# w1's last 64 rows on 16 partitions, by one transfer with an outermost dimension of 4

## The chip, the cores and the metric

The kernel runs on one core of one Trainium2 chip. The metric is the device time of one execution in microseconds (us); lower is better.

## The reference, cut to what matters

The result is `x + A(xn) + B(xn)`. A is a decode attention over a window of 2048 keys and values (16 K and 16 V transfers of 2 MB each in the kernel; they are most of the 88.5 MB read). B is a small MLP, and the change is in its first matrix, w1:

```python
h = _gelu(_layernorm(x, axis=-1) @ w1)          # x: 4 x 1 x 576, w1: 576 x 576
c = D // 4
g0 = jnp.pad(h[:, :, 0*c:1*c], ((0, 0), (1, 0), (0, 0)))[:, :S, :]
...                                             # g1, g2, g3 likewise: shifts along S by 1 and 2
hs = jnp.concatenate([g0, g1, g2, g3], axis=-1) @ w2
x1 = x + hs
h2 = _gelu(_layernorm(x1, axis=-1) @ w3) @ w4
```

S is 1 here. A shift by one or two positions leaves padding alone, so `hs` is zero whatever h is. The kernel nevertheless loads w1 and w2 and computes h and hs. Two things follow. The output can't tell whether h is right, so the correctness test says nothing of the new layout of w1. And in an experiment h may be wrong while the output stays right.

## The kernel before: the parts that matter

All large transfers are issued by SP on one queue, in the order of the `key` at the end of each line; in the trace each large one has 16 landings, one for each of the core's 16 DMA engines, and each engine works through its own share of the queue without a gap (its next packet starts 3 to 4 ns before the last one ends). Of each 576-row matrix, 512 rows fill 128 partitions with four rows each; the last 64 rows ("rag") are interleaved on the even and the odd partitions of a shared tile.

```python
def rag_pair(tile, even, odd):
    return [(tile[p:128:2, 0:w.shape[1]], w[512:576, :]) for p, w in enumerate((even, odd))]
...
ev_wq = [add_dma([(kt_t[:], A_wq[0:512, :].rearrange("(p r) n -> p (r n)", r=4))], "wq", (), -60),
         add_dma(rag_pair(ragq3, B_w3, A_wq), "wqr", ["ragq3_zero"], -59)]
ev_r12 = add_dma(rag_pair(rag12, B_w1, B_w2), "r12", (), -58.5)
ev_w2 = add_dma([(w2main, B_w2[0:512, :].rearrange("(p r) n -> p r n", r=4))], "w2", (), -58)
ev_w3 = add_dma([(w3_t[:], B_w3[0:512, :].rearrange("(p r) n -> p (r n)", r=4))], "w3", (), -57)
ev_w1 = add_dma([(w1main, B_w1[0:512, :].rearrange("(p r) n -> p r n", r=4))], "w1", (), -56)
...                                 # then K0 to K15, V0 to V15, wo, and w4 in five pieces
def pe_h(h):                        # x @ w1, for one half of the columns
    def f(e):
        for r in range(4):
            e.matmul(HTps[h], lhsT=xn2T[:, r, :], rhs=w1main[:, r, HALF * h:HALF * (h + 1)], start=(r == 0), stop=False)
        return e.matmul(HTps[h], lhsT=xn2T[:, 4, :], rhs=rag12[:, HALF * h:HALF * (h + 1)], start=False, stop=True)
    return f
```

Of the kernel before, what the change touches and what calls it, by code (L numbers as in the profile page):

```python
# [7 lines left out]
BF16 = mybir.dt.bfloat16  # L8
# [27 lines left out]
def bass_parallel_sum__sliding_block_cached__mixer_s_mlp__decode_kernel(  # L36
    nc, A_x, A_k_cache, A_v_cache, A_wq, A_wo, B_x, B_w1, B_w2, B_w3, B_w4, out
):
    B, Sq, D = A_x.shape
# [14 lines left out]
    HALF = D // 2  # L54
# [5 lines left out]
    with ExitStack() as ctx:  # L60
        def sb(name, shape, dt):
            return ctx.enter_context(nc.sbuf_tensor(name, shape, dt))
# [7 lines left out]
        w4_t = sb("w4", [128, 36 * D], BF16)  # L70
# [15 lines left out]
        w2main = w4_t[:, 4 * D:8 * D].rearrange("p (r n) -> p r n", r=4)  # L86
        rag12 = w4_t[:, 8 * D:9 * D]
        ragq3 = w4_t[:, 9 * D:9 * D + F]

        x_sb = sb("x_sb", [B, D], BF16)  # L90
        stats = sb("stats", [B, 3, 2, 6], FP32)
# [6 lines left out]
        x1n_bf = sb("x1n_bf", [B, D], BF16)  # L98
        ragsrc = sb("ragsrc", [B, 3, 128], BF16)
        xnT = sb("xnT", [128, 5, 32], BF16)  # L100
        xn2T = sb("xn2T", [128, 5, B], BF16)
        x1nT = sb("x1nT", [128, 5, 32], BF16)
        hs_inT = sb("hs_inT", [128, 5, B], BF16)
        h_sb = sb("h_sb", [B, D], BF16)
# [6 lines left out]
        ident_bf = sb("ident_bf", [128, 128], BF16)  # L111
# [20 lines left out]
        ps = ctx.enter_context(nc.psum_tensor("ps", [128, 8, 512], FP32))[:]  # L132
# [11 lines left out]
        H2Tb = ps[:, 6, :].bitcast(BF16)[:, 0:128]  # L144
        HSps = [ps[0:B, k, 0:HALF] for k in range(2)]
        HTps = [ps[0:B, 2 + k, 0:HALF] for k in range(2)]
        XTps = [ps[:, k, a:a + 10].bitcast(BF16).rearrange("p (c b) -> p c b", b=B) for k, a in ((3, 300), (7, 0), (7, 12))]

        S = {}
        for nm in ("pe", "dve", "act", "pool"):  # L150
# [5 lines left out]
        def add(engine, emit, waits=(), sig=None, key=0.0, inc=(), loop=None, cond=None):  # L156
            seqc[0] += 1
            prog[engine].append(Op(emit, waits, sig, key, seqc[0], inc, loop, cond))

        def tok(nm):  # L160
            if nm not in S:
                S[nm] = sem("t_" + "_".join(str(k) for k in (nm if isinstance(nm, tuple) else (nm,))))
            return nm
# [6 lines left out]
        def add_dma(pairs, skey, waits=(), key=0.0, engine="sp"):  # L170
            tok(skey)
            dma_count[skey] = dma_count.get(skey, 0) + 16 * len(pairs)

            def emit(e):
                for o_, i_ in pairs:
                    e.dma_start(o_, i_).then_inc(S[skey], 16)  # L176
            add(engine, emit, waits, None, key)
            return ("dma", skey, dma_count[skey])

        def rag_pair(tile, even, odd):  # L180
            return [(tile[p:128:2, 0:w.shape[1]], w[512:576, :]) for p, w in enumerate((even, odd))]
# [6 lines left out]
        P = lambda *a, **k: add("pool", *a, **k)  # L188

        def pool_ident(t, tag, pattern, view, key):  # L190
            P(lambda e: e.memset(t[:], 1.0), sig=tag + "1", key=key)
            P(lambda e: e.affine_select(out=view, in_=view, compare_op=ALU.is_equal, fill=0.0, base=0,
                                        pattern=pattern, channel_multiplier=1), waits=[tag + "1"], sig=tag, key=key + 0.5)
        P(lambda e: e.memset(ragq3[:, Hq * Dh:F], 0.0), sig="ragq3_zero", key=-101)
        P(lambda e: e.memset(zeros_bf[:], 0.0), sig="zeros_bf", key=-100)
        pool_ident(ident_bf, "ident_bf", [[-1, 128]], ident_bf[:], -99)
        P(lambda e: e.memset(ragsrc[:], 0.0), sig="rag_zero", key=-97)
        P(lambda e: e.memset(Qpad_t[:], 0.0), sig="qpad_zero", key=-96)
# [12 lines left out]
            waits=["ident_f"], sig="mU", key=-8)  # L211
        for x in range(2):
# [3 lines left out]
        ev_x = add_dma([(x_sb[:], x2)], "x", ["sqrt_table"], -100, engine="act")  # L216
        ev_wq = [add_dma([(kt_t[:], A_wq[0:512, :].rearrange("(p r) n -> p (r n)", r=4))], "wq", (), -60),
                 add_dma(rag_pair(ragq3, B_w3, A_wq), "wqr", ["ragq3_zero"], -59)]
        ev_r12 = add_dma(rag_pair(rag12, B_w1, B_w2), "r12", (), -58.5)
        ev_w2 = add_dma([(w2main, B_w2[0:512, :].rearrange("(p r) n -> p r n", r=4))], "w2", (), -58)  # L220
        ev_w3 = add_dma([(w3_t[:], B_w3[0:512, :].rearrange("(p r) n -> p (r n)", r=4))], "w3", (), -57)
        ev_w1 = add_dma([(w1main, B_w1[0:512, :].rearrange("(p r) n -> p r n", r=4))], "w1", (), -56)
# [32 lines left out]
        def ln_ops(idx, src, dst, first_waits, tag, k0):  # L255
            add("dve", lambda e: (e.bn_stats(out=stats[:, idx, 0, :], in_=src[:, 0:HALF]),
                                  e.bn_stats(out=stats[:, idx, 1, :], in_=src[:, HALF:D]))[1],
                waits=first_waits, sig=f"{tag}_st", key=k0)
            add("dve", lambda e: e.bn_aggr(out=mv[:, idx, :], in_=stats[:, idx].rearrange("p a s -> p (a s)")),  # L259
                waits=[f"{tag}_st"], sig=f"{tag}_mv", key=k0 + 0.01)  # L260
            add("act", lambda e: e.activation(out=sd[:, idx:idx + 1], in_=mv[:, idx, 1:2], func=ACTF.Sqrt, bias=EPS, scale=1.0),  # L261
                waits=[f"{tag}_mv"], sig=f"{tag}_sd", key=k0 + 0.02)
            add("dve", lambda e: e.reciprocal(out=rstd[:, idx:idx + 1], in_=sd[:, idx:idx + 1]),
                waits=[f"{tag}_sd"], sig=f"{tag}_rstd", key=k0 + 0.03)
            add("dve", lambda e: e.tensor_scalar(out=dst[:], in0=src[:], scalar1=mv[:, idx, 0:1], scalar2=rstd[:, idx:idx + 1],
                                                 op0=ALU.subtract, op1=ALU.mult), waits=[f"{tag}_rstd"], sig=f"{tag}_n", key=k0 + 0.04)
            odd = int(idx == 0)
            add("dve", lambda e: e.tensor_copy(out=ragsrc[:, idx, odd:128:2], in_=dst[:, 512:D]), waits=[f"{tag}_n", "rag_zero"], sig=tag, key=k0 + 0.05)  # L268

        def pe_xT(src, idx):  # L270
            def f(e):
                v = src[:, 0:512].rearrange("b (p r) -> b r p", r=4)
                for r in range(4):
                    e.transpose(XTps[idx][:, r, :], v[:, r, :], ident_bf[0:B, 0:B])  # L274
                return e.transpose(XTps[idx][:, 4, :], ragsrc[:, idx, :], ident_bf[0:B, 0:B])
            return f

        ln_ops(0, x_sb, xn_bf, [ev_x], "ln1", -40)
        ln_ops(1, xn_bf, xn2_bf, ["ln1"], "ln2", -30)
        add("pe", pe_xT(xn_bf, 0), waits=["ident_bf", "ln1"], sig="xT", key=-40)  # L280
        add("dve", lambda e: e.tensor_copy(out=xnT[:, :, 0:B], in_=XTps[0]), waits=["xT", "xnT_zero"], sig="xnT", key=-39)

        def pe_q(r):
            def f(e):
# [25 lines left out]
        for b in range(B):  # L310
            add("dve", lambda e, b=b: e.tensor_copy(out=qp_out[:, b], in_=qp_in[:, b]), waits=["qTp", "qpad_zero"],
                sig="qT" if b == B - 1 else None, key=-29.4)
        add("pe", pe_xT(xn2_bf, 1), waits=["ln2", "ident_bf"], sig="x2T", key=-36)
        add("dve", lambda e: e.tensor_copy(out=xn2T[:], in_=XTps[1]), waits=["x2T"], sig="xn2T", key=-25)

        def pe_zero(e):
            ins = None
# [37 lines left out]
        for c in range(NC):  # L355
            lp = ("K", c // NPOS)
            for k in range(NBLK):
# [4 lines left out]
                eng, f = evac(NBLK * c + k)  # L362
                add(eng, f, waits=[f"T{NBLK * c + k}"] + ([f"SC{c - 2}"] if c >= 2 else []), inc=[("evA" if eng == "act" else "evD", 1)],
                    key=NBLK * c + k + 0.2)
            add("pe", pe_SC(c - 1), waits=[take("qs")], sig=f"SC{c - 1}", key=NBLK * c + SC_AFTER + 0.5, loop=lp)
            b, gq = CH[c]
            cc = 4 * b + gq
            P(lambda e, c=c, cc=cc: e.tensor_copy(out=Qs[:, c % NPOS, :], in_=Qpad_t[:, 128 * cc:128 * cc + 128]),  # L368
              waits=["qT", "qs_zero"] + ([f"SC{c - NPOS}"] if c >= NPOS - 1 else []), inc=[("qs", 1)], key=c)
# [6 lines left out]
            waits=["rmax"], sig="negb", key=KS + 0.05)  # L376
        for q in range(4):
            add("act", lambda e, q=q: e.activation(out=P_sb[:, q, :], in_=Sps[:, q, :], func=ACTF.Exp,
                                                   bias=negb[:, 0:1], scale=scale, accum_out=rs4[:, q:q + 1]),
                waits=["negb"], sig=f"exp{q}", key=KS + 0.1 + 0.01 * q)  # L380

        for q in range(4):
            k0 = KS + 0.2 + 0.1 * q
            add("dve", lambda e, q=q: e.transpose(out=PTx[:, q, :], in_=P_sb[:, q, :]), waits=[f"exp{q}"], sig=f"PTx{q}", key=k0)  # L384
            add("pe", lambda e, q=q: e.matmul(ps[:, 4 + q % 3, :], lhsT=permT_bf[:], rhs=PTx[:, q, :], start=True, stop=True),  # L385
                waits=[f"PTx{q}", "permT_bf"] + (["PT0"] if q == 3 else []), sig=f"PTy{q}", key=k0)
            add("act", lambda e, q=q: e.activation(out=PT_t[:, 512 * q:512 * (q + 1)], in_=ps[:, 4 + q % 3, :], func=ACTF.Copy),
                waits=[f"PTy{q}"], sig=f"PT{q}", key=k0 + 0.16)
# [3 lines left out]
            waits=["rinv", "ident_f"], sig="diag", key=KS + 0.82)  # L392
        add("pe", lambda e: e.matmul(rinvps, lhsT=ones_f[:], rhs=diag[:], start=True, stop=True), waits=["diag", "ones_f", "exp3"],
            sig="rinvp", key=KS + 0.9)
        add("dve", lambda e: e.tensor_copy(out=rinvB[:].rearrange("p (c u e) -> p c u e", u=NU, e=2),
                                           in_=rinvps.rearrange("p (u c e) -> p c u e", u=NU, e=2)),
            waits=["rinvp"], sig="rinvB", key=KS + 1.5)
# [20 lines left out]
        for c in range(NC):  # L418
            w = [f"PV{c - 2}"] if c >= 2 else [f"PT{q}" for q in range(4)] + ["mU_bf1"]
            b, gq = CH[c]  # L420
            add("dve", dve_pad(c), waits=w, inc=[(tok("pad"), 1)], key=KV + 2 * max(c - 1, 0) + 0.2)
            add("pe", pe_PV(c), waits=[take("pad"), take(("v", c % NPOS), 16)] + ([take("otn")] if b == 0 else []), sig=f"PV{c}",
                key=KV + 2 * c, loop=("V", gq))
            if b == B - 1:
                hv = lambda t, gq=gq: t[:, 0:128].rearrange("p (b h) -> p b h", b=B)[:, :, 8 * gq:8 * gq + 8]
                add("dve", lambda e, hv=hv: e.tensor_tensor(out=hv(OTn), in0=OTps.rearrange("p (b h) -> p b h", b=B), in1=hv(rinvB), op=ALU.mult),  # L426
                    waits=["rinvB", f"PV{c}"], sig=f"OTn{gq}" if gq == 3 else None, inc=[(tok("otn"), 1)] if gq < 3 else [], key=KV + 2 * c + 0.1)
# [13 lines left out]
        def pe_AO(half):  # L441
# [10 lines left out]
            waits=["OTy"], sig="ORp", key=KT - 2.5)  # L452
# [15 lines left out]
        def pe_h(h):  # L468
            def f(e):
                for r in range(4):  # L470
                    e.matmul(HTps[h], lhsT=xn2T[:, r, :], rhs=w1main[:, r, HALF * h:HALF * (h + 1)], start=(r == 0), stop=False)
                return e.matmul(HTps[h], lhsT=xn2T[:, 4, :], rhs=rag12[:, HALF * h:HALF * (h + 1)], start=False, stop=True)
            return f
        for h in range(2):
            add("pe", pe_h(h), waits=[ev_w1, ev_r12, "xn2T", "xnT"], sig=f"hT{h}", key=-3 + 0.1 * h)
# [7 lines left out]
        for h in range(2):  # L483
# [3 lines left out]
                waits=[f"hs{h}", "ln1"], sig="x1" if h else "x1a", key=-29 + 0.6 * h)  # L487
        ln_ops(2, x1_bf, x1n_bf, ["x1"], "ln3", -24)
        add("dve", lambda e: e.tensor_tensor(out=t1[:], in0=x_sb[:], in1=x1_bf[:], op=ALU.add), waits=["x1"], sig="t1", key=-5)
        add("pe", pe_xT(x1n_bf, 2), waits=["ln3", "xn2T"], sig="x1T", key=-23)  # L490
        add("dve", lambda e: e.tensor_copy(out=x1nT[:, :, 0:B], in_=XTps[2]), waits=["x1T", "x1nT_zero"], sig="x1nT", key=-23)
        for h in range(2):
            add("act", lambda e, h=h: e.activation(out=h_sb[:, HALF * h:HALF * (h + 1)], in_=HTps[h], func=ACTF.Gelu_apprx_tanh),
                waits=[f"hT{h}", "x1nT"], sig="gelu_h" if h else None, key=-0.69 + 0.01 * h)

        segs = []
        for g in range(4):
            t = 9 * g
            while t < 9 * g + 9:
                n = next(m for m, (a, z) in enumerate(W4N) if a <= t < z)  # L500
# [18 lines left out]
        for k in range(3):  # L519
            add("act", lambda e, k=k: e.activation(out=h2g[:, 9 * XS[k]:9 * XS[k + 1]], in_=H2ps[k], func=ACTF.Gelu_apprx_tanh), waits=["h2_3"],  # L520
                sig="gelu2" if k == 2 else None, key=-0.9 + 0.1 * k)

        def pe_h2T(e):
# [7 lines left out]
            waits=["h2T"], inc=[("evA", 1)], key=-0.3)  # L531
        add("dve", lambda e: e.tensor_copy(out=h2o[:, :, 8, :], in_=H2Tb.rearrange("p (g y) -> p g y", g=4)[..., 0:B]),
            waits=["h2T"], inc=[("evD", 1)], key=-0.3)
# [112 lines left out]
```

## Time and profile before

The median was 214.85 us of 3 runs (214.82 to 215.07).

| | before | read from |
|---|---|---|
| span | 213.6 us | page |
| DMA engines, mean rate | 415 GB/s | page, part 2 and the DMA line |
| last step of the chain | 32.2 us of DMA, w4 | chain of waits |
| tensor engine busy | 67% | page, part 1 |
| K transfer, issue to landing | 14.5 us | DMA issues |

The page's rows for the DMA in 40 slices of the span (tenths busy, then GB/s), and its DMA line:

```profile
DMA  7999989999999999999999999999999999999993
GB/s 270 418 380 507 442 359 436 417 428 423 426 430 426 423 430 436 422 430 426 433 426 430 430 422 427 430 420 433 430 423 426 430 433 426 426 429 439 422 406 130
DMA packets 6546, 88.65 MB, mean 415 GB/s; under 512 B 764, under 2 KB 1032, under 8 KB 1544
```

The chain that ended last, in order of time (start in us, length in us, what):

```profile
178.05 0.04 issue
178.09 32.22 DMA w<-in_B_w_dram
210.31 0.04 issue
210.36 1.40 PE ps L431 x18
211.75 0.43 DVE out_sb L548
```

The reader is to see two things. The DMA is busy from the second slice to the last but one. And the end waits for the last piece of w4, issued 32 us earlier, which lay behind everything else on the queue. The kernel is bound by the DMA queue: its packets fill 97.8% of the 16 engines' span.

One level lower, the trace records each DMA packet with start, length and size. A packet of one size nearly always took the same time: 51 ns for 1152 B, 178 ns for 4608 B, 611 ns or a little more for 16384 B; the next packet on its engine started 3 to 4 ns before it ended. So each engine's end is the sum of its packets. The engines don't end together: the 16 landings of each transfer late in the run are spread over 2.0 us. This is the table of landings of two transfers, in ns after the first engine's landing (below I call this an engine's phase), computed from the packet records (K0 is the first K transfer, V15 the last V transfer):

```
before, K0  at  33.82 us: 0 31 66 133 159 162 244 289 308 338 389 449 450 451 492 1711
before, V15 at 191.03 us: 0 5 13 155 245 410 427 898 1440 1525 1628 1664 1691 1895 1964 2020
```

Most of the spread comes from fetches of instructions. Queue 8, of the kind "instruction", moved 8 packets of 16 KB, seven of them before the last pieces of w4; each took 1.02 to 1.10 us on one engine, stretched a packet beside it as well, and set that engine back by 1.5 us against the others (1711 in the first row is one: this engine stood at 172 when wq had landed). So each fetch costs time on the DMA engine that carries it among the data; what it costs the engine whose instructions are fetched I did not measure.

### The profile page before, as it was taken

How to read it: one execution, taken by the hardware profiler on the slowest of the kernel's cores; microseconds unless marked ns; L12 is line 12 of the kernel's file. 1: busy time of each engine (PE TensorE's matmuls, PEld its weight loads, DVE VectorE, ACT ScalarE, POOL GpSimd, SP SyncE). 2: the span in 40 equal slices, each digit the busy share in tenths (PEclk: the TensorE clock that was granted, in tenths of full speed). 3: DMA queues.
4: the chain of work that ended last, by engine and by line, in shares of the span. 5: the costliest groups of instructions: out<-in, count | busy, mean ns of one | idle time of the engine just before them, and what ended most of it. 6: DMA issues, size and time to landing. Idle time of an engine off the chain costs nothing. (4 is left out here: it accounts for less than half of the span.)

```text
span 213.6 us, 5903 instructions
## 1 busy us (share of the span) xinstructions
PE 142.3 (67%) x2664; PEld 110.4 (52%) x2668; DVE 75.2 (35%) x147; ACT 61.8 (29%) x76; POOL 10.9 (5%) x38
## 2 busy tenths in 40 slices
PE   0058469999999999999996178033444433336995
PEld 0023256877778887888874058033434433334542
DVE  0332701666666666666664840100010001001000
ACT  2001204666555665666666530000000000000000
POOL 8301000000000000000000000000000000000000
PEclk9999959999999999999999555555555555555799
DMA  7999989999999999999999999999999999999993
GB/s 270 418 380 507 442 359 436 417 428 423 426 430 426 423 430 436 422 430 426 433 426 430 430 422 427 430 420 433 430 423 426 430 433 426 426 429 439 422 406 130
DMA packets 6546, 88.65 MB, mean 415 GB/s; under 512 B 764, under 2 KB 1032, under 8 KB 1544
## 3 DMA queue, kind: packets, MB, share of 16 engines
q1 hardware_dynamic: 6520, 88.50, 97.8%
q8 instruction: 8, 0.13, 0.2%
q14 instruction: 2, 0.02, 0.0%
q10 hardware_dynamic: 16, 0.01, 0.0%
HBM read 88.49 MB, written 0.00 MB: 414 GB/s over the span
## 5 line engine op out<-in xcount | busy, mean ns | idle before, releaser
L333 PE MATMUL ps<-perm_bf,ring 128*128 128x128 bf16 x1024 | 62.5, 219 | 1.3 <-PEq L572 0.3
L333 PEld LDWEIGHTS ps<-perm_bf,ring 128*128 128x128 bf16 x1024 | 57.5, 98 | 10.7 <-issue 10.7
L340 DVE COPY kt<-ps 128x1024 bf16<-128x1024 bf16 x80 | 52.3, 687 | 27.2 <-PE ps L333 27.2
L339 ACT ACTIVATE kt<-ps 128x1024 bf16<-128x1024 bf16 x48 | 49.2, 1024 | 30.8 <-PE ps L333 29.5
L414 PE MATMUL ps<-PTpad,ring 128*128 128x8 bf16 x1024 | 29.6, 168 | 41.2 <-PEq L572 37.6
L414 PEld LDWEIGHTS ps<-PTpad,ring 128*128 128x128 bf16 x1024 | 28.7, 104 | 42.3 <-issue 42.2
L549 ACT ACTIVATE out_sb<-ps 4x288 bf16<-4x288 f32 x1 | 0.4, 402 | 87.2 <-PE ps L431 87.2
L347 PE MATMUL ps<-kt,Qs 128*32 128x512 bf16 x272 | 17.8, 382 | 1.4 <-PEq L572 1.4
L403 DVE TENSOR_TENSOR PTpad<-PT,mU_bf 128x512 bf16<-128x512 bf16 x16 | 6.4, 421 | 29.4 <-PE ps L414 29.4
L426 DVE TENSOR_TENSOR OTn<-ps,rinvB 128x32 bf16<-128x32 f32 x4 | 0.8, 191 | 34.5 <-PE ps L414 34.5
L347 PEld LDWEIGHTS ps<-kt,Qs 128*32 128x32 bf16 x272 | 5.7, 95 | 6.8 <-issue 1.5
L274 PE MATMUL ps<-ident_bf,xn_bf 4*128 4x4 bf16 x8 | 0.6, 170 | 12.9 <-DVE ragsrc L268 12.9
L368 POOL COPY Qs<-Qpad 128x128 bf16<-128x128 bf16 x16 | 4.6, 296 | 86.9 <-PE ps L347 73.6
L511 PE MATMUL ps<-w,x1nT 128*32 128x387 bf16 (+7 forms) x90 | 5.9, 404 | 2.3 <-DMA w<-in_B_w_dram 2.0
L274 PEld LDWEIGHTS ps<-ident_bf,xn_bf 4*128 4x128 bf16 x8 | 0.4, 112 | 12.9 <-issue 10.5
L511 PEld LDWEIGHTS ps<-w,x1nT 128*32 128x32 bf16 x90 | 4.5, 124 | 3.6 <-DMA w<-in_B_w_dram 2.3
L431 PE MATMUL ps<-w,ORT 128*4 128x288 bf16 x64 | 5.5, 345 | 0.4 <-DVE ORT L453 0.4
L548 DVE CAST out_sb<-ps 4x288 bf16<-4x288 f32 x1 | 0.4, 446 | 14.5 <-PE ps L431 14.5
L431 PE MATMUL ps<-w,h2T_sb 128*4 128x288 bf16 x72 | 5.0, 286 | 0.7 <-DMA w<-in_B_w_dram 0.7
L385 PE MATMUL ps<-kt,permT_bf 128*128 128x512 bf16 x3 | 1.8, 607 | 4.9 <-DVE kt L384 4.8
L261 ACT ACTIVATE sd<-mv 4x1 f32<-4x1 f32 x3 | 0.6, 202 | 14.8 <-DVE mv L259 14.8
L431 PEld LDWEIGHTS ps<-w,ORT 128*4 128x4 bf16 x64 | 3.3, 102 | 2.9 <-DVE ORT L453 1.0
(99 smaller groups left out, 65.8 us busy)
## 6 DMA issues: line engine op xcount, KB each, us to landing
ring<-in_A_k_cache_dram SPq DMA_DIRECT2D x16, 2048.0 KB, 14.5
ring<-in_A_v_cache_dram SPq DMA_DIRECT2D x16, 2048.0 KB, 17.4
w<-in_B_w_dram SPq DMA_DIRECT2D x1, 4608.0 KB, 24.0
w<-in_A_wo_dram SPq DMA_DIRECT2D x2, 2304.0 KB, 20.9
kt<-in_A_wq_dram SPq DMA_DIRECT2D x1, 4096.0 KB, 12.3
w<-in_B_w_dram SPq DMA_DIRECT2D x1, 2592.0 KB, 28.0
w<-in_B_w_dram SPq DMA_DIRECT2D x3, 576.0 KB, 13.7
w<-in_B_w_dram SPq DMA_DIRECT2D x1, 1296.0 KB, 30.6
```

The lines of the kernel that those rows point to most:

```text
L274: e.transpose(XTps[idx][:, r, :], v[:, r, :], ident_bf[0:B, 0:B])
L333: ins = e.transpose(tb[n % 4][:, t, :], slot_t(c)[:, 8 * k + t, :], perm_bf[:])
L339: return "act", lambda e: e.activation(out=ktbuf[:, n % 16], in_=tb[n % 4], func=ACTF.Copy)
L340: return "dve", lambda e: e.tensor_copy(out=ktbuf[:, n % 16], in_=tb[n % 4])
L347: ins = e.matmul(Sps[32 * u:32 * u + 32, q, :].rearrange("p (t i) -> p t i", t=16), lhsT=Qs[:, c % NPOS, 32 * u:32 * u + 32], rhs=ktgrp[:, ...
L368: P(lambda e, c=c, cc=cc: e.tensor_copy(out=Qs[:, c % NPOS, :], in_=Qpad_t[:, 128 * cc:128 * cc + 128]), waits=["qT", "qs_zero"] + ([f"SC{ ...
L385: add("pe", lambda e, q=q: e.matmul(ps[:, 4 + q % 3, :], lhsT=permT_bf[:], rhs=PTx[:, q, :], start=True, stop=True), waits=[f"PTx{q}", "pe ...
L403: return lambda e: e.tensor_tensor(out=PTpad[:, c % 2], in0=PTv[:, :, cc, :].unsqueeze(2).to_broadcast([128, NT, NU, 2]), in1=mU_bf[:].uns ...
L414: ins = e.matmul(o_, lhsT=slot_t(c)[:, t, :], rhs=PTpad[:, c % 2, t].rearrange("p u e -> p (u e)"), start=(t == 0), stop=(t == NT - 1))
L426: add("dve", lambda e, hv=hv: e.tensor_tensor(out=hv(OTn), in0=OTps.rearrange("p (b h) -> p b h", b=B), in1=hv(rinvB), op=ALU.mult), waits ...
L431: return e.matmul(ACC[h], lhsT=lhsT, rhs=rhs, start=start, stop=stop, tile_position=(0, 32 * h), skip_group_check=True)
L511: ins = e.matmul(H2ps[k][32 * g:32 * g + 32, :].rearrange("p (x c) -> p x c", c=9)[:, :, off:off + cnt], lhsT=x_, rhs=w[:, base_:base_ + 1 ...
```

## The change

Its intent: replace 64 small packets by 16 large ones that occupy four engines only. Rows are chosen so that partition 4a+b gets the four neighbouring rows 16b+4a to 16b+4a+3, that is 4608 contiguous bytes; the source's outermost dimension is 4. The matmul that consumed 64 (of 128) partitions becomes four matmuls on 16 partitions, and x is transposed to fit. "w3 whole ahead of w1" holds in both kernels: those lines are not touched. The diff, cut to its core:

```diff
+        w1rag = w4_t[0:16, 18 * D:22 * D]
...
-        xn2T = sb("xn2T", [128, 5, B], BF16)
+        xn2T = sb("xn2T", [128, 8, B], BF16)
...
+        P(lambda e: e.memset(rag12[:], 0.0), sig="rag12_zero", key=-98)
...
-        ev_r12 = add_dma(rag_pair(rag12, B_w1, B_w2), "r12", (), -58.5)
+        ev_r12 = add_dma([(w1rag, B_w1[512:576, :].rearrange("(b a c) n -> a b (c n)", b=4, a=4)),
+                          (rag12[1:128:2, :], B_w2[512:576, :])], "r12", ["rag12_zero"], -58.5)
...
+            if idx == 1:
+                r_out = ragsrc[:, idx, 0:64].rearrange("q (c a b) -> q c a b", c=4, a=4)
+                r_in = r_in.rearrange("q (b a c) -> q c a b", b=4, a=4)
...
+                for c in range(4):
+                    ins = e.transpose(XTps[idx][0:16, 4 + c, :], ragsrc[:, idx, 16 * c:16 * c + 16], ident_bf[0:B, 0:B])
...
-                return e.matmul(HTps[h], lhsT=xn2T[:, 4, :], rhs=rag12[:, HALF * h:HALF * (h + 1)], start=False, stop=True)
+                for c in range(4):
+                    ins = e.matmul(HTps[h], lhsT=xn2T[0:16, 4 + c, :], rhs=w1rag[:, c * D + HALF * h:c * D + HALF * (h + 1)], start=False, stop=(c == 3))
+                return ins
```

More of the change, by code (lines that the diff above doesn't have):

```diff
@@ L146, in bass_parallel_sum__sliding_block_cached__mixer_s_mlp__decode_kernel @@
         HTps = [ps[0:B, 2 + k, 0:HALF] for k in range(2)]
-        XTps = [ps[:, k, a:a + 10].bitcast(BF16).rearrange("p (c b) -> p c b", b=B) for k, a in ((3, 300), (7, 0), (7, 12))]
+        XTps = [ps[:, k, a:a + 16].bitcast(BF16).rearrange("p (c b) -> p c b", b=B) for k, a in ((3, 300), (7, 0), (7, 20))]
         S = {}
@@ L266, in ln_ops @@
                                                  op0=ALU.subtract, op1=ALU.mult), waits=[f"{tag}_rstd"], sig=f"{tag}_n", key=k0 + 0.04)
-            odd = int(idx == 0)
-            add("dve", lambda e: e.tensor_copy(out=ragsrc[:, idx, odd:128:2], in_=dst[:, 512:D]), waits=[f"{tag}_n", "rag_zero"], sig=tag, key=k0 + 0.05)
+            r_out, r_in = ragsrc[:, idx, int(idx == 0):128:2], dst[:, 512:D]
+            if idx == 1:
+                r_out = ragsrc[:, idx, 0:64].rearrange("q (c a b) -> q c a b", c=4, a=4)
+                r_in = r_in.rearrange("q (b a c) -> q c a b", b=4, a=4)
+            add("dve", lambda e: e.tensor_copy(out=r_out, in_=r_in), waits=[f"{tag}_n", "rag_zero"], sig=tag, key=k0 + 0.05)
         def pe_xT(src, idx):
@@ L274, in f @@
                     e.transpose(XTps[idx][:, r, :], v[:, r, :], ident_bf[0:B, 0:B])
-                return e.transpose(XTps[idx][:, 4, :], ragsrc[:, idx, :], ident_bf[0:B, 0:B])
+                if idx != 1:
+                    return e.transpose(XTps[idx][:, 4, :], ragsrc[:, idx, :], ident_bf[0:B, 0:B])
+                for c in range(4):
+                    ins = e.transpose(XTps[idx][0:16, 4 + c, :], ragsrc[:, idx, 16 * c:16 * c + 16], ident_bf[0:B, 0:B])
+                return ins
             return f
@@ L280, in bass_parallel_sum__sliding_block_cached__mixer_s_mlp__decode_kernel @@
         add("pe", pe_xT(xn_bf, 0), waits=["ident_bf", "ln1"], sig="xT", key=-40)
-        add("dve", lambda e: e.tensor_copy(out=xnT[:, :, 0:B], in_=XTps[0]), waits=["xT", "xnT_zero"], sig="xnT", key=-39)
+        add("dve", lambda e: e.tensor_copy(out=xnT[:, :, 0:B], in_=XTps[0][:, 0:5, :]), waits=["xT", "xnT_zero"], sig="xnT", key=-39)
         def pe_q(r):
@@ L313, in bass_parallel_sum__sliding_block_cached__mixer_s_mlp__decode_kernel @@
         add("pe", pe_xT(xn2_bf, 1), waits=["ln2", "ident_bf"], sig="x2T", key=-36)
-        add("dve", lambda e: e.tensor_copy(out=xn2T[:], in_=XTps[1]), waits=["x2T"], sig="xn2T", key=-25)
+        add("dve", lambda e: e.tensor_copy(out=xn2T[:, 0:4, :], in_=XTps[1][:, 0:4, :]), waits=["x2T"], sig=None, key=-25)
+        add("dve", lambda e: e.tensor_copy(out=xn2T[0:16, 4:8, :], in_=XTps[1][0:16, 4:8, :]), waits=["x2T"], sig="xn2T", key=-24.9)
         def pe_zero(e):
@@ L471, in f @@
                     e.matmul(HTps[h], lhsT=xn2T[:, r, :], rhs=w1main[:, r, HALF * h:HALF * (h + 1)], start=(r == 0), stop=False)
-                return e.matmul(HTps[h], lhsT=xn2T[:, 4, :], rhs=rag12[:, HALF * h:HALF * (h + 1)], start=False, stop=True)
+                for c in range(4):
+                    ins = e.matmul(HTps[h], lhsT=xn2T[0:16, 4 + c, :], rhs=w1rag[:, c * D + HALF * h:c * D + HALF * (h + 1)], start=False, stop=(c == 3))
+                return ins
             return f
@@ L490, in bass_parallel_sum__sliding_block_cached__mixer_s_mlp__decode_kernel @@
         add("pe", pe_xT(x1n_bf, 2), waits=["ln3", "xn2T"], sig="x1T", key=-23)
-        add("dve", lambda e: e.tensor_copy(out=x1nT[:, :, 0:B], in_=XTps[2]), waits=["x1T", "x1nT_zero"], sig="x1nT", key=-23)
+        add("dve", lambda e: e.tensor_copy(out=x1nT[:, :, 0:B], in_=XTps[2][:, 0:5, :]), waits=["x1T", "x1nT_zero"], sig="x1nT", key=-23)
         for h in range(2):
```

## The prediction

> What bounds the kernel now: the DMA queue. The page's slice row shows the DMA engines at 9 tenths or more from the second slice to the last but one; the chain that ended last is one DMA step of 32.2 us (15%, the last piece of w4). In the trace's packet records the 16 engines run back to back (a packet starts 3 to 4 ns before the last one ends); a packet's time depends on its size alone: 1152 B 51 ns, 4608 B 178 ns, 16384 B 611 to 614 ns. So the total is set by the engine with the most packet time. The engines don't end together: the last piece's 16 landings spread from 220.7 to 222.7 us of the trace's clock, about 2 us, because each 16 KB instruction fetch (queue 8) takes one engine's slot and sets it back by about 1.5 us.
>
> What the change moves. Before, w1's last rows are 64 packets of 1152 B, four on each of 16 engines, about 193 ns each (4 x 47 + 5 for the semaphore). After, they are 16 packets of 4608 B. [...] The trace agrees for x (4 rows: four packets, on four engines). I estimate 4 x 174 + 5 = 0.70 us[...]. Net: +0.51 us on four engines, -0.19 us on twelve. The order w2, w3, w1 on the queue is already that of before, so nothing is won from it.
>
> Is one of the four a late engine? By the phases left after x's packets, the four sit at about 160, 290, 390 and 490 ns in the first order of landings; the last in that order (490) is among those that a fetch delays, and is probably the very last at the end. Then the end moves by about +0.5 us. If the fetches fall otherwise, the twelve decide, and the end moves by -0.2 to 0 us.
>
> Off the critical path: 6 more matmuls (three more for each half of h, 0.12 to 0.14 us each) and 3 more transposes, one more DVE copy (0.15 us), one more POOL memset (an estimated 0.6 us, from 0.53 us for 128x512) ahead of the issue of r12. The memset ends near 2.9 us, while the queue has wq until 12 us. The first K transposes (36.3 us) come about 0.7 us later. K slots are issued 14.5 us before they land, three transfers of 4.9 us each, so the DMA stays fed and that work costs nothing.
>
> Predicted 215.15 us (+0.3), between +0.5 (six in ten) and -0.2 to 0 (four in ten); range 214.5 to 215.6. Same within 2%: 0.97; faster 0.01; slower 0.02.
>
> What the profile would show: 16 packets of 4608 B more and 64 of 1152 B less; w1's rest landing about 0.5 us later on four engines; the spread between first and last landing of the following transfers wider by up to 0.7 us until the end; no gap in the DMA; later first transposes, without effect on K's landing. Wrong would be: a transfer spread over 16 engines (then no change), other fetches than before, small packets that cost more than their size, or K transfers issued so late that the DMA idles.

0.70 us less 0.19 us is +0.51 us on four engines, -0.19 us on twelve, and 214.85 us (the median before) plus 0.3 us is 215.15 us. What the trace before shows is the transfer of x: four rows, four packets of 1152 B, four semaphore writes, while a transfer spread over all engines has 16. That the new transfer would do likewise was an estimate from this one case.

## The result, and the profile after

The changed kernel took 214.69 us (median of 6 runs, 214.67 to 214.91), the kernel before 214.96 us (6 runs, 214.81 to 215.13). The ratio is 0.9989, with a 95% interval of 0.9976 to 1.0002. A ratio here is the mean time of one kernel's runs over that of the other's in the same rounds, so it is not quite the ratio of the medians quoted. At a threshold of 2% this is "same"; the interval holds a gain of 0.5 us as well as none.

The same lines of the page after:

```profile
DMA  7999999999999999999999999999999999999993
GB/s 276 412 384 483 435 390 433 427 425 424 421 430 433 424 430 430 429 421 436 424 433 424 424 432 428 421 427 430 424 427 430 421 436 427 433 422 438 428 403 143
DMA packets 6486, 88.65 MB, mean 415 GB/s; under 512 B 752, under 2 KB 956, under 8 KB 1484
```

and the chain that ended last:

```profile
177.77 0.04 issue
177.81 32.24 DMA w<-in_B_w_dram
210.06 0.04 issue
210.10 1.39 PE ps L442 x18
211.49 0.43 DVE out_sb L561
```

The shape is that of before, 0.25 us earlier. Not all of this is the change: the first landing of wq, ahead of the transfer that was changed, already came at 12.156 us instead of 12.281, and over all traces it lies anywhere from 12.107 to 12.368 us. There are 60 packets fewer: 64 of 1152 B and 12 semaphore writes are gone, 16 of 4608 B have come. The twelve missing semaphore writes are those of engines that have no part in the transfer any more: it did run on four.

The packet records give a clean measure of what this costs the others. I take the time from the first engine's landing of wq (the first transfer) to the first engine's landing of K0; the last rows of w3 and wq, then r12, w2, w3, w1 and K0 lie between, and no instruction fetch has reached the engine that is first there. It is 21.543 us before and 21.350 us after: 193 ns less, to the nanosecond what one 4 x 1152 B share takes (4 x 47 + 5). The landings after:

```
after, K0  at  33.51 us: 0 136 173 177 246 327 439 480 499 534 553 | 879 992 1050 1083 | 1797
after, V15 at 190.72 us: 0 166 235 487 531 811 993 1492 1644 1651 1727 1762 1930 1999 2018 2055
```

In K0 the group between the bars is the four engines of the new transfer: they are the ones that also carried x's four packets, and each had four packets of 4608 B. (The bars are mine.) They are 0.70 us behind where they would be among the others. At the end the last engine is still 2.06 us behind the first, as before, and it is none of the four: it is an engine that stood at 534 ns in K0 and was set back by a 16 KB fetch at 40.1 us.

On the tensor engine h takes longer, too. These are the matmuls around h before (L471 and L472 are h; start in us, length in us), followed by the transposes of h2 and the first transposes of K:

```profile
33.00 0.28 PE L471 MATMUL ps<-w,xn2T 128*4 128x288 bf16 x1
...
34.10 0.29 PE L472 MATMUL ps<-w,xn2T 128*4 128x288 bf16 x1
34.77 0.77 PE L526 MATMUL ps<-ident_bf,PT 128*128 128x128 bf16 x9 [0.39 <-ACT PT L520]
...
36.36 0.22 PE L333 MATMUL ps<-perm_bf,ring 128*128 128x128 bf16 x1
```

and after (L482 and L484 are h):

```profile
33.38 0.40 PE L482 MATMUL ps<-w,xn2T 128*4 128x288 bf16 x1
...
34.16 0.65 PE L484 MATMUL ps<-w,xn2T 16*4 16x288 bf16 x4
34.74 0.65 PE L482 MATMUL ps<-w,xn2T 128*4 128x288 bf16 x4
35.32 0.65 PE L484 MATMUL ps<-w,xn2T 16*4 16x288 bf16 x4
35.90 0.77 PE L539 MATMUL ps<-ident_bf,PT 128*128 128x128 bf16 x9
...
37.36 0.22 PE L344 MATMUL ps<-perm_bf,ring 128*128 128x128 bf16 x1
```

h takes from 33.38 to 35.97 us, 2.6 us, against 1.4 us before (33.00 to 34.39), and the first transposes of K come 1.0 us later. Not all of it is the six added matmuls. Run e11_four_at_0 below has the new transfer and the old matmuls: there h starts at 33.38 us as well and ends at 35.15, and the first transposes of K start at 36.91. So the matmuls account for 0.8 us of h and 0.45 us of the transposes' delay. Nothing of that reaches the end. The time from issue to landing of a K transfer is the last figure of these lines, before and after:

```profile
ring<-in_A_k_cache_dram SPq DMA_DIRECT2D x16, 2048.0 KB, 14.5
```

```profile
ring<-in_A_k_cache_dram SPq DMA_DIRECT2D x16, 2048.0 KB, 14.4
```

So the queue stays as full as it was.

### The profile page after: what moved, and what is told of

Read it like the earlier page. It is cut to its first block, busy times and chain, and to the rows that moved or that the text cites. A ratio compares the mean times of both kernels' runs of the same rounds, so it can differ in the third digit from the quotient of the medians.

```text
span 213.4 us, 5927 instructions
## 1 busy us (share of the span) xinstructions
PE 144.7 (68%) x2677; PEld 111.4 (52%) x2677; DVE 75.2 (35%) x148; ACT 61.4 (29%) x76; POOL 11.4 (5%) x39
## 5 line engine op out<-in xcount | busy, mean ns | idle before, releaser
L350 ACT ACTIVATE kt<-ps 128x1024 bf16<-128x1024 bf16 x48 | 48.6, 1023 | 30.0 <-PE ps L344 29.0
L524 PE MATMUL ps<-w,x1nT 128*32 128x387 bf16 (+7 forms) x90 | 6.4, 420 | 1.3 <-DMA w<-in_B_w_dram 1.0
L442 PE MATMUL ps<-w,ORT 128*4 128x288 bf16 x64 | 6.1, 370 | 0.4 <-DVE ORT L464 0.4
L396 PE MATMUL ps<-kt,permT_bf 128*128 128x512 bf16 x4 | 2.4, 608 | 4.3 <-DVE kt L395 4.1
```

What stands on the lines that cost most here:

```text
L350: return "act", lambda e: e.activation(out=ktbuf[:, n % 16], in_=tb[n % 4], func=ACTF.Copy)
L396: add("pe", lambda e, q=q: e.matmul(ps[:, 4 + q % 3, :], lhsT=permT_bf[:], rhs=PTx[:, q, :], start=True, stop=True), waits=[f"PTx{q}", "pe ...
L442: return e.matmul(ACC[h], lhsT=lhsT, rhs=rhs, start=start, stop=stop, tile_position=(0, 32 * h), skip_group_check=True)
L524: ins = e.matmul(H2ps[k][32 * g:32 * g + 32, :].rearrange("p (x c) -> p x c", c=9)[:, :, off:off + cnt], lhsT=x_, rhs=w[:, base_:base_ + 1 ...
```

## The experiments

Theory A: the time is that of the slowest DMA engine; the change takes 0.19 us from twelve engines and puts it, and more, on four that have room, so the end comes 0.19 us earlier as long as none of the four becomes the last. Rival P: fewer and larger packets are the gain. Rival L: the new layout and its matmuls have a share. Rival N: there is no difference. The first results brought a further theory, Q: the partitions that a transfer writes matter as well, and packets to the wrong ones hold up those behind them. The expectations below were written before their runs.

In all these tables, "wq to K0" is the measure from above (first landing to first landing, from the packet records), and "stretched" counts the 128 packets of 4608 B of w2 (and those of w1's rest, where it has this size) that took over 200 ns instead of 178.

| run | ratio to before | 95% interval | median us (before) | wq to K0, us | stretched |
|---|---|---|---|---|---|
| changed kernel, first rounds | 0.9989 | 0.9976 to 1.0002 | 214.69 (214.96) | 21.350 | 0 |
| a0_after | 0.9994 | 0.9981 to 1.0008 | 214.91 (215.06) | 21.349 | 0 |
| e1_sixteen | 1.0020 | 1.0006 to 1.0033 | 215.50 (215.06) | 22.047 | 46 |
| e2_old_layout_four | 1.0007 | 0.9993 to 1.0020 | 215.16 (215.06) | 21.605 | 33 |
| e6_rest_not_loaded | 0.9992 | 0.9978 to 1.0005 | 214.93 (215.06) | 21.350 | 0 |
| e3_four_twice | 1.0022 | 1.0008 to 1.0036 | 215.56 (215.03) | 21.358 | 0 |
| e4_two_engines | 1.0040 | 1.0026 to 1.0053 | 215.91 (215.03) | 21.349 | 7 |
| e5_pe_later | 1.0002 | 0.9989 to 1.0016 | 215.11 (215.03) | 21.543 | 0 |
| e7_no_w1_w2 | 0.9851 | 0.9836 to 0.9867 | 211.81 (215.03) | | |
| e8_32_spread | 1.0001 | 0.9987 to 1.0014 | 214.95 (214.94) | 21.536 | 0 |
| e9_32_low | 1.0020 | 1.0007 to 1.0034 | 215.30 (214.94) | 21.778 | 38 |
| e10_four_at_64 | 1.0029 | 1.0015 to 1.0043 | 215.57 (214.94) | 21.951 | 65 |
| e11_four_at_0 | 0.9998 | 0.9985 to 1.0012 | 214.84 (214.94) | 21.349 | 0 |

All outputs were correct. In the traces of the kernel before and of e5_pe_later, which leave this transfer as it was, the measure is 21.543 us both times. (In e3_four_twice the engine that is first in wq is one of the four, and the next one lands 8 ns later; hence 21.358.)

### a0_after: the changed kernel again

No edit.

> The changed kernel again, in more rounds. Theory A (the end is set by an engine outside the four that got w1's rest; each of those lost 4 packets of 1152 B, about 0.19 us): ratio to before 0.9990 to 0.9993, that is 0.15 to 0.22 us less, and the last landing of w4's last piece on one of the twelve. Theory N (no real difference, noise of 0.1 to 0.3 us): ratio 0.9997 to 1.0003.

Measured: ratio 0.9994, in the gap between the two expectations; both comparisons lie under 1, but each interval includes 1. The times alone don't settle 0.2 us, so they don't refute rival N. The trace repeats to a nanosecond: 21.349 us. The last landing of V15 (2.13 us after the first) is again that of an engine outside the four.

### e6_rest_not_loaded: without the transfer

```diff
-        ev_r12 = add_dma(rag_pair(rag12, B_w1, B_w2), "r12", (), -58.5)
+        ev_r12 = add_dma([(rag12[1:128:2, :], B_w2[512:576, :])], "r12", ["rag12_zero"], -58.5)
```

(and the memset of rag12 as in the change; h is wrong.)

> The kernel before, without the load of w1's last 64 rows (zeros stand in their place; h is wrong, but the output doesn't depend on it). Theory A: all sixteen engines lose 0.19 us, the end comes 0.19 us earlier, as in the changed kernel, which would then hide the whole transfer; ratio 0.9989 to 0.9993. If the four engines still cost something in the changed kernel, this one is faster than it by more than 0.05 us. Theory N: ratio 1.

Measured: ratio 0.9992, wq to K0 21.350 us. On the twelve engines that set the end, the changed kernel is as if w1's rest were not loaded at all. The two medians, 214.91 and 214.93 us, came from the same rounds.

### e3_four_twice: twice the load on the four

```diff
+                          (w4_t[0:16, 22 * D:26 * D], B_w1[512:576, :].rearrange("(b a c) n -> a b (c n)", b=4, a=4)),
```

> The changed kernel, with w1's rest loaded a second time by the same four-engine transfer into unused space: 0.70 us more on each of the four, nothing on twelve. Theory A: in the changed kernel's trace the latest of the four stands 0.04 us before the last engine, so now it is the last, and the end moves by 0.6 to 0.7 us: 0.4 to 0.5 us over before, ratio 1.0018 to 1.0026. Rival B (the sum of bytes over all engines decides): 0.18 us more, ratio 0.9998 to 1.0002. Rival S (the four have slack for more): as the changed kernel.

Measured: ratio 1.0022, that is 0.5 us over before and 0.6 to 0.7 us over the changed kernel. The sum of bytes would have given 0.18 us, and slack nothing. In the landings one engine now stands alone at the end; before the second load it was one among several. It is one of the four: the one at 1718 in the first row, which a short (8 KB) fetch at 47.0 us then set back by 0.97 us.

```
e3_four_twice, K0  at  33.73 us: 0 30 111 133 142 175 201 223 291 302 389 1396 1477 1528 1600 1718
e3_four_twice, V15 at 190.93 us: 0 39 114 158 200 1445 1460 1509 1581 1587 1594 1665 1922 2028 2043 2701
```

This run with e6 shows the mechanism: the first 0.70 us on four engines cost nothing that shows (a0_after and e6, 214.91 and 214.93 us), and the second 0.70 us, with one of the four now the last, cost nearly in full (0.6 to 0.7 us). It also says how near the changed kernel is to that point: one of its four was 0.04 to 0.06 us before the last in the first trace (0.24 us or a little more in that of a0_after).

### e1_sixteen: one packet for each of 16 engines

```diff
-        ev_r12 = add_dma([(w1rag, B_w1[512:576, :].rearrange("(b a c) n -> a b (c n)", b=4, a=4)),
+        ev_r12 = add_dma([(w1rag, B_w1[512:576, :].rearrange("(a c) n -> a (c n)", c=4)),
```

(and x's columns in the order to match.)

> As changed (16 packets of 4608 B, same matmuls, same POOL memset), but the source's outermost dimension is 16 instead of 4, so one packet for each of 16 engines. Theory A: each engine has 0.18 us where before had 0.19, so the time is that of before (ratio 0.9997 to 1.0003), about 0.18 us over the changed kernel. Rival P (the gain came from fewer and larger packets): time as the changed kernel or less, ratio 0.9988 to 0.9993. Landings of the next transfers again in one band of about 0.5 us, without a group of four 0.7 us behind.

Measured: ratio 1.0020, neither theory: 0.4 us slower than before. The sum of packet times alone falls. P predicted a gain and there is none, but a second effect came in, so this is no clean test of P. wq to K0 took 0.50 us more than before. The packet records show that w1's packets took their 178 ns, but those behind them did not: packets of w2's rest took up to 148 ns instead of 51, and packets of w2 up to 427 ns. The windows of the DMA show the dip. First the kernel before (columns: window in us; then its length; busy time of each engine; granted clock; DMA share; GB/s), then this run:

```profile
14.00:15.00 1.00, 1.00 (x16) 0.32 (x8) 0.00 (x0) 0.00 (x0) 0.00 (x0) 1.00 0.97 408
15.00:16.00 1.00, 1.00 (x16) 0.36 (x12) 0.00 (x0) 0.00 (x0) 0.00 (x0) 1.00 1.06 408
```

```profile
14.00:15.00 1.00, 0.72 (x12) 0.50 (x16) 0.19 (x2) 0.00 (x0) 0.00 (x0) 1.00 0.97 408
15.00:16.00 1.00, 1.00 (x16) 0.39 (x12) 0.00 (x0) 0.00 (x0) 0.00 (x0) 1.00 1.05 270
```

The DMA share stays at 1.05 while the rate falls to 270 GB/s: the engines are as busy, with packets that take longer. What differs from the transfer before is the size of the packets and the destination: partitions 0 to 15, where it was 64 partitions from 0 to 126. Against e6_rest_not_loaded, where no such packets run, wq to K0 takes 0.697 us more (22.047 less 21.350). An estimate from the trace: that is as much as four packets of 4608 B in a row, at 174 ns from one packet's start to the next, though each engine carried only one. Why it is so much, the trace does not show. That the destination is the cause became theory Q, which e8 to e11 test.

### e2_old_layout_four: the old layout on four engines

```diff
-        ev_r12 = add_dma(rag_pair(rag12, B_w1, B_w2), "r12", (), -58.5)
+        ev_r12 = add_dma([(rag12[0:128:2, :], B_w1[512:576, :].rearrange("(b a) n -> a b n", a=4)),
+                          (rag12[1:128:2, :], B_w2[512:576, :])], "r12", (), -58.5)
```

(and x's columns in the order to match.)

> The kernel before with its old layout and its five matmuls, and w1's last rows still as 64 packets of 1152 B, but with the source's outermost dimension 4: 16 packets for each of four engines, none for twelve. Theory A: twelve engines lose 0.19 us, the four gain 16 x 47 + 5 - 193 = 0.56 us; time 0.15 to 0.22 us under before (or a tie with the latest of the four). Rival P (packet size) and rival L (the new layout on the tensor engine): as before, ratio 0.9997 to 1.0003.

Measured: ratio 1.0007, wq to K0 21.605 us, 33 packets stretched. A miss: the twelve did not get their 0.19 us (the time to K0 even grew by 0.06 us), although the transfer ran on four engines (four landings of K0 stand 0.7 us behind the rest). Its 64 rows go to 64 partitions from 0 to 126, those of the changed kernel to partitions 0 to 15, from four engines in both. That fits Q but doesn't prove it, as the packets' size differs too, and the run says nothing about P or L.

### e8, e9, e10 and e11: the same transfer to other partitions

All four are e6_rest_not_loaded plus a transfer of w1's rest into space that nobody reads; only the destination and the split differ. The matmuls are those of the kernel before.

```diff
e8:  +  (w4_t[0:128:4, 18 * D:20 * D], B_w1[512:576, :].rearrange("(a c) n -> a (c n)", c=2)),
e9:  +  (w4_t[0:32,    18 * D:20 * D], B_w1[512:576, :].rearrange("(a c) n -> a (c n)", c=2)),
e10: +  (w4_t[64:80,   18 * D:22 * D], B_w1[512:576, :].rearrange("(b a c) n -> a b (c n)", b=4, a=4)),
e11: +  (w4_t[0:16,    18 * D:22 * D], B_w1[512:576, :].rearrange("(b a c) n -> a b (c n)", b=4, a=4)),
```

> The kernel before, with w1's rest brought to 32 partitions 0, 4, ..., 124 (two packets of 2304 B on each of 16 engines) and read by nobody (h wrong, output right). Theory Q [...]: [...] from the first landing of wq to the first landing of K0 21.35 + 0.18 = 21.53 us, time as before, ratio 0.9997 to 1.0003. Rival D (spreading this transfer over 16 engines disturbs the reads, whatever the destination): near 22.0 us and ratio 1.0015 to 1.0025.

> The same with partitions 0 to 31[...]. Theory Q: [...] from wq to K0 about 21.7 us and packets of w2 behind it stretched; 0.15 to 0.2 us over the spread one, ratio 1.0004 to 1.0012. Rival D: no difference from the spread one.

> The kernel before, with w1's rest by four engines as in the change, but to partitions 64 to 79, read by nobody. Theory Q: [...] besides the four, four more engines lose time there (stretched packets of w2), and the first landing of K0 stays at 21.35 us after wq; with a fetch on one of those the end comes 0.2 to 0.5 us later than in the next run. Rival: as the next run.

> The same to partitions 0 to 15, as the change has it, but with the matmuls of before. Theory A with Q: no packet stretched, 21.35 us from wq to K0, time as the changed kernel, ratio 0.9988 to 0.9996. Rival L (the new matmuls and layout have a share in the changed kernel's time): differs from it by over 0.1 us.

The 21.7 us of e9 were 21.35 + 0.36, and the 0.36 is the time of four packets of 2304 B in a row (93 ns each in the trace before, 89 from start to start), and that four would queue was not shown.

Measured, e8 against e9: the same source, the same 16 engines, two packets of 2304 B on each; one goes to partitions 0, 4, ..., 124, the other to partitions 0 to 31. e8: 21.536 us (21.53 expected), no packet stretched, ratio 1.0001. e9: 21.778 us (21.7 expected), 38 packets stretched, ratio 1.0020. So the spread over 16 engines does no harm by itself, and D falls; the destination does. e8 is also the test that e1 had failed to be: larger packets (2304 B), evenly spread, with none stretched, bring back the time of before (21.536 and 21.543 us). P falls here. e9's ratio lies above the 1.0004 to 1.0012 expected and is more than its 0.24 us in the trace explain, but its interval reaches down to 1.0007.

e11 against e10: the same four engines and packets, only other partitions. e11 has 21.349 us and no stretched packet, as the changed kernel; e10 has 21.951 us and 65 stretched packets, ratio 1.0029. The windows again, e11 and then e10:

```profile
15.00:16.00 1.00, 1.00 (x12) 0.32 (x8) 0.00 (x0) 0.00 (x0) 0.00 (x0) 1.00 1.02 405
16.00:17.00 1.00, 1.00 (x16) 0.44 (x12) 0.00 (x0) 0.00 (x0) 0.00 (x0) 1.00 1.77 747
```

```profile
15.00:16.00 1.00, 1.00 (x16) 0.46 (x12) 0.00 (x0) 0.00 (x0) 0.00 (x0) 1.00 1.14 343
16.00:17.00 1.00, 1.00 (x16) 0.32 (x8) 0.00 (x0) 0.00 (x0) 0.00 (x0) 1.00 1.00 313
```

(The 747 in the second window of e11 is a matter of bookkeeping, as in the kernel before with 723: the packets of w3, 36 KB each, start there and are counted where they start.)

The choice of partitions 0 to 15 for four engines is therefore part of the change's gain. Why these partitions and not those is not shown: the packet records name neither the engine nor the partition. One part of my expectation for e10 was wrong: I expected four more engines to suffer, and the first landing of K0 came 0.60 us later, on all of the twelve. Why every engine is slowed is open. So what the runs show is that the destination decides (0.24 us between e8 and e9, 0.60 us between e11 and e10), not by what means.

As to rival L, e11 has the old matmuls and the new transfer: its ratio, 0.9998, is outside the 0.9988 to 0.9996 expected, but it and those of the changed kernel, 0.9994 and 0.9989, don't differ beyond their intervals. The times can't say more; the traces agree to a nanosecond up to K0.

### e4_two_engines: the load on two engines

```diff
-        ev_r12 = add_dma([(w1rag, B_w1[512:576, :].rearrange("(b a c) n -> a b (c n)", b=4, a=4)),
+        ev_r12 = add_dma([(w1rag, B_w1[512:576, :].rearrange("(b a c) n -> a b (c n)", b=8, a=2)),
```

> The changed kernel with the source's outermost dimension 2: eight packets of 4608 B on each of two engines (1.4 us each), 14 engines none. In the changed kernel's trace the four end 1.25, 1.05, 0.57 and 0.04 us before the last. Theory A: [...] the move of another 0.70 us onto them costs nothing and the time stays 0.15 to 0.22 us under before; if one of the two is the latest of the four, 0.4 to 0.5 us over before. Rival B: as the changed kernel whichever they are.

Measured: ratio 1.0040, 0.9 us over before, the worst of all. The first of the fourteen has its 21.349 us. One of the two needed 1.39 us for its eight packets, the other 1.88 us, and two further engines lost about half a microsecond each; seven packets of w2 were stretched here as well. One of the two was already the last engine in K0, 2.65 us behind the first, and a short instruction fetch (8 KB, at 88.7 us) set it back by another 0.7 us. Rival B, by which the placement doesn't matter, falls, though the stretched packets keep this run from being as clean as e3; the size is beyond what I had expected because of the packets that took longer (1.88 us for eight, where eight took 1.39 us on the other engine) and of that fetch.

### e5_pe_later: later first transposes

```diff
-            for q in range(4):
+            for q in (0, 1, 2, 3) * 3:
```

(in the zero matmuls ahead of the first K transposes of the kernel before.)

> The kernel before, with 8 more zero matmuls (about 1.7 us) ahead of the first transposes. Theory A: the queue is three transfers ahead, so the time is that of before, ratio 0.9997 to 1.0003. Rival T (the later first transposes cost something, so that the changed kernel's gain is a larger one less such a cost): 0.3 us or more slower, ratio above 1.0010.

Measured: ratio 1.0002. The first transposes started at 38.1 us, 1.8 us later than before, and nothing came of it. So I see no cost of the changed kernel's 1.0 us there, and rival T finds no support; the interval alone, which reaches to 1.0016, would not exclude a small one.

### e7_no_w1_w2: without w1 and w2

This one follows from the reference, not from the change: with S = 1, hs is zero, so x1 = xn. The edit takes out the three transfers (r12, w2, w1), the matmuls of h and hs and the activation of h, and copies xn to x1:

```diff
-        ev_r12 = add_dma(rag_pair(rag12, B_w1, B_w2), "r12", (), -58.5)
-        ev_w2 = add_dma([(w2main, B_w2[0:512, :].rearrange("(p r) n -> p r n", r=4))], "w2", (), -58)
-        ev_w1 = add_dma([(w1main, B_w1[0:512, :].rearrange("(p r) n -> p r n", r=4))], "w1", (), -56)
...
-            add("dve", lambda e, cs=cs, h=h: e.tensor_tensor(out=x1_bf[:, cs], in0=HSps[h], in1=xn_bf[:, cs], op=ALU.add),
+            add("dve", lambda e, cs=cs, h=h: e.tensor_copy(out=x1_bf[:, cs], in_=xn_bf[:, cs]),
```

> The kernel before without any load of w1 and w2 and without the work on them: with one position per sequence the shifted h is padding alone (the kernel's hs_inT is zero and never written), so the output needs neither. Theory A: each engine loses 2 x (8 x 174 + 5) + 2 x 193 = 3.2 us, all of it from the end: 211.6 to 211.9 us, ratio 0.984 to 0.986, output still right. If the startup's chain on the other engines becomes the limit, less than 2 us.

Measured: 211.81 us, ratio 0.9851, in the expected range: 3.2 us of packets removed from every engine are 3.2 us of time. It beats both kernels. It is right for one position per sequence (and finite weights) alone, and it drops work instead of doing it better; whether that is allowed is the owner's decision.

## Why the prediction was right or wrong

The measured 214.69 us lies in the stated range (214.5 to 215.6), and "same within 2%" came true. The middle of it was wrong in sign: I gave six chances in ten to +0.5 us, and the other branch, -0.2 to 0 us, came.

- What bounds the kernel: right. The DMA queue is never empty, and removing packet time from all engines (e7) or adding it to the last one (e3) moved the end by about that (3.2 us and 0.6 to 0.7 us).
- The number of engines: right. I expected four for the change, whose source has an outermost dimension of 4, and the trace shows four engines 0.70 us behind, each with four packets of 4608 B more than the others. With 2 (e4) and 16 (e1) the landings show two and 16. The runs show it for these cases only.
- The size of the shift, +0.51 us on four and -0.19 us on twelve: right. 193 ns were measured on the twelve.
- Which branch: wrong. The step that failed is "the last in that order (490) is among those that a fetch delays, and is probably the very last at the end". The engine at 492 ns was delayed, but by a short fetch (8 KB, at 47.1 us), which set it back by 0.97 us, to 1462 ns. The 16 KB fetch 0.6 us later hit another engine with nearly the same phase (451 ns), and that one became the last, at 2001 ns. I had seen both engines leave the list of early ones at the same K transfer and had taken the wrong one. Following single packets from engine to engine, instead of the sorted lists, would have told them apart. In the changed kernel's first trace the same holds: the short fetch went to one of the four, and the first three long ones went to others.

  In the kernel before, that engine of the four stood 0.54 us before the last. This is less than the change moves the four against the twelve, 0.70 us (0.51 and 0.19): by that trace, as an estimate, it would have become the last by 0.16 us, and nearly all of the gain would have gone. In the changed kernel's first trace the latest of the four still had 0.04 to 0.06 us, in a0_after 0.24 us, because the engines stood otherwise to each other when the fetches came. That the last engine was none of the four was therefore luck in part, by a margin that I had not computed.

  There is a pattern that I overlooked: in the traces of the changed kernel, a0_after, e3 and e10, both short fetches (near 47 and 88 us) went to two of the four, and no long one up to V15 did. A short one sets back by 0.7 to 1.0 us, a long one by 1.5 us, and this difference gives the four their room; why the fetches are dealt out so is open. (In the trace of the kernel before, one long fetch, at 159.0 us, can't be told between one of the four and an engine of the same phase.)
- The tensor engine's share: right (no effect on the end: e5). I estimated 0.8 us for the six matmuls, and against e11, which starts h at the same time, they took 0.8 us (35.97 less 35.15); the rest of the 1.2 us (2.6 less 1.4) is in e11 as well. The K transposes came 1.0 us later, not 0.7.
- What I did not see at all: the destination. The prediction counted packets for each engine and took their time as given by the size. That fails where the destination stretches them (46, 38 and 65 packets of 4608 B in e1, e9 and e10 took over 200 ns instead of 178). For the change itself it made no difference, as none of its packets was stretched; for another placement it would have (e10, 0.60 us).

What stays open: whether there is a gain in the mean, and whether it is 0.1 or 0.25 us. The trace gives 0.193 us up to K0. From there to the last data packet of w4 the traces of the unhindered kernels took between 177.17 us (e11) and 177.40 us (e6), probably because the phase of the engines that the fetches meet differs from run to run. A gain that small can be shown in the packet records up to K0 but hardly in the times.

## What to carry to other kernels

When a kernel is bound by a DMA queue, ask which engine ends last, not how many bytes move: a small transfer that is put on engines with room (here an outermost dimension of 4 of the source did it) was free until one of them became the last (0.70 us on four engines, a0_after and e6), and then it cost nearly in full (0.6 to 0.7 us of another 0.70 us, e3). Look at two things, the load of each engine and the partitions that are written: from wq to K0 a transfer from 16 engines to partitions 0 to 15 took 0.50 us more than the kernel before and 0.70 us more than the changed kernel, which loads the same partitions from four engines (e1), one to partitions 0 to 31 took 0.24 us more than the same one spread over SBUF (e9, e8), and one from four engines to partitions 64 to 79 took 0.60 us more than to 0 to 15 (e10, e11). And before tuning a load, ask whether the output depends on it: leaving out w1 and w2 was worth 3.2 us, hiding w1's last rows 0.19 us at the most.
